# Attention and gated MLP on one core: earlier places in the queues for attention's sums, x's casts and the root's first step

## The chip, the core and the metric

The kernel runs on one core of a Trainium2 chip. Its time is the device time of one launch in microseconds (us). The core has a TensorE (PE, with a queue of weight loads PEld beside the matmuls), a VectorE (DVE), a ScalarE (ACT), a GpSimd (POOL) and a SyncE (SP), which issues the transfers. Each engine carries out its own instructions strictly in order; they wait for each other by semaphores. So the order in which instructions stand in an engine's queue is all that this change can act on.

## The reference

```python
# attention: B, H, S, D = 8, 8, 576, 64; two kinds of sparse causal mask
scores = np.where(masks, scale * q @ k.T, -1e9)      # window 32, or 32 keys at a distance of 4
attn = np.exp(scores - max); attn = attn / (sum + 1e-09)
x = (attn @ v)  ->  4608 tokens x 512
# MLP
rms = np.sqrt(np.mean(x * x, axis=-1, keepdims=True) + 1e-06)
xn = x / rms * rms_g
g = xn @ w_gate                                       # 512 x 1536
silu = g * (1.0 / (1.0 + np.exp(-g)))
return silu * (xn @ w_val) @ w_out                    # 1536 x 512
```

## The kernel before

The 4608 tokens are cut into 16 units `u` of 288 tokens. The MLP of a unit goes through 12 blocks `j` of 128 hidden columns. Each block has three **ticks**: the gate tick (PE: `g`, 12 matmuls), the val tick (PE: `v`, 12 matmuls) and the proj tick (PE: the products of the block before with `w_out`, 12 matmuls into `acc`). A unit is thus a stage of 36 ticks, about 67 us. Twelve matmuls stand for four products, since every operand is held as a sum of a rounded high part and a low part in fp32r and three of the four partial products are taken; this is why there are pairs `xhi, xlo`, `hhi, hlo`, `vhl`, `pt[:, 0], pt[:, 1]`.

Attention for unit u + 1 runs in the gaps of unit u's MLP. It has 14 bursts (a block of queries of two heads) per unit, one every second tick. A burst passes through: scores `s` on PE; maximum on DVE (`scores_max`, L379 and L384); exponential on ACT (L395); sum and reciprocal on DVE (L404, L405); scaling on GpSimd (L411); transpose `t` on PE (L482); the transposed probabilities are cast to a high part on ACT (L462) and their low part is taken on DVE (`low_part`, L464); product with v on PE (`o`, L494); and `take` (L432, L434, twice) sums the partial outputs on DVE into `xraw`.

PE's order in a tick is: the tick's 12 matmuls, then the products of attention (`o` first, then `t`, then `s`). What the other engines do with a tick's results is put off by `later(dt, rank, fn)` to the start of a tick dt ticks on, where `flush` carries out all that is due there in the order of the ranks. So a smaller rank means a place further ahead in the engines' queues, within one tick. `now[0]` counts the ticks; `ends` is the number of the first tick of the MLP, which is a proj tick, so `(now[0] - ends) % 3 == 0` names proj ticks. The argument `wait` of `products` is 1 in gate ticks, 2 in val ticks and 0 in proj ticks: what was issued in a proj tick is worked on at the start of the next gate tick.

PSUM is scarce: `g` and `v` of successive blocks alternate between two banks, and a transpose shares one with them. A transpose of a proj tick lies in the bank of `g` of its block j, and that is also the bank of `v` of block j + 1:

```python
    def bank(kind, j):
        return "gv"[(j + (kind == "v")) % 2]
```

So PE may write `v` of block j + 1 only when both ACT (L462) and DVE (L464) have read that transpose. Likewise a transpose of a val tick lies in the bank of that block's `g`, and PE may write it only when DVE's silu (`th` L690) has read `g`. `th` itself has a single buffer: ACT's tanh (L685) of a block waits until GpSimd has made `hlo` of the block before (L715).

At the end of a unit's attention `rms_sum` adds up squares on PE, `rms_root` makes 1/rms (DVE L559, then on GpSimd L560 the power, L565 and L566 the two parts), `spread` puts the parts on diagonals (`rd`, DVE L574 and ACT L578), and `rms_apply` broadcasts them by two matmuls into `bps` (L594). Then for each of four 128-row chunks c, `normal` scales x (DVE L608), and `part` splits it (ACT L625 `xhi`; low part L626 `xlo`, on GpSimd for even c and on DVE for odd c). The parts of chunks 0 and 3 fall into proj ticks.

Of the kernel before, what the change touches and what calls it, by code (L numbers as in the profile page):

```python
# [29 lines left out]
NEX = 3  # L30
# [46 lines left out]
def attn_moe(ctx: ExitStack, tc: tile.TileContext, qk_in, v_in, w_gate, w_val, w_out, rms_g, outT):  # L77
# [38 lines left out]
    now = [0]  # L116
    put_off = {}

    def later(dt, rank, fn):
        put_off.setdefault(now[0] + dt, []).append((rank, fn))  # L120
# [294 lines left out]
    def take(u, c, i, o):  # L415

        blocks, nq, _ = geometry(u, c)
        if (u, c) not in xraw:
            xraw[u, c] = sb.tile([P, U], F32, tag="xraw", name=f"xraw_{u}_{c}", bufs=NC)
        x = xraw[u, c]  # L420
        if c < NC // 2:
            to = x[:, QB * i:QB * i + nq]
        else:
            to = x.rearrange("p (j r) -> p r j", r=DIL)[:, i, :]
        copy = V.tensor_copy if i % 2 and u == 0 and c == NC - 1 else A.copy
        if u < NEX:
            for a in range(2):
                copy(out=to[a * D:(a + 1) * D], in_=o[a * D:(a + 1) * D, a * nq:(a + 1) * nq])
        else:
            for a in range(2):  # L430
                ours, cols = to[a * D:(a + 1) * D], 2 * a * nq
                V.tensor_reduce(out=ours, in_=o[:D, cols:cols + 2 * nq].rearrange("d (t q) -> d q t", t=2),  # L432
                                axis=mybir.AxisListType.X, op=ALU.add)
                V.tensor_tensor(out=ours, in0=o[D:, cols:cols + nq], in1=ours, op=ALU.add)  # L434
        if i == len(blocks) - 1:
            dt = 1 if c != 1 or u < NEX else 4
            later(dt, 0.44 if u >= NEX and (now[0] + dt - ends) % 3 == 0 else 2.5 if u else 1.9, lambda: square(u, c))
# [31 lines left out]
    def products(q, t, o, t_ps, s_tag="s", o_tag="o", wait=0):  # L469


        if q:
            s_ps = ps.tile([P, 512], F32, tag=s_tag, name=f"s_{q[0]}_{q[1]}_{q[2]}")
        if o:
            o_ps = ps.tile([P, 512], F32, tag=o_tag, name=f"o_{o[0]}_{o[1]}_{o[2]}")
            pt = st.pop(o)
        if t:
            p, _ = st.pop(t)
        def transposed(a):
            blocks, nq, _ = geometry(*t[:2])  # L480
            n = blocks[t[2]][3]
            PE.transpose(t_ps[:n, a * QB:a * QB + nq], p[:nq, a, :n], ident[:nq, :nq])  # L482

        def output(a):
            blocks, nq, _ = geometry(*o[:2])
            n = blocks[o[2]][3]
            if o[0] < NEX:
                if a:
                    return
                out = o_ps[:, :2 * nq].rearrange("d (a q) -> d a q", a=2)  # L490
                PE.matmul(out, vs.pop(o)[:n].rearrange("k a d -> k (a d)"), pt[:n, 0, :, :nq], start=True, stop=True)
                return
            vp = vparts[everything.index(o) % 2]
            PE.matmul(o_ps[:, 2 * a * nq:2 * (a + 1) * nq].rearrange("d (t q) -> d t q", t=2),  # L494
                      vp[:n, a].rearrange("k t d -> k (t d)"), pt[:n, :, a, :nq], start=True, stop=True)

        def scored(a):
            blocks, nq, _ = geometry(*q[:2])
            qc, kc, _, n = blocks[q[2]]
            sv = s_ps[:QB].rearrange("q (a t k) -> q a t k", a=2, t=2)  # L500
            if q[0] < NEX:
                qk = heads[q[0], 2 * q[1] + a]
                PE.matmul(sv[:nq, a, 0, :n], qk[:, qc:qc + nq], qk[:, U + kc:U + kc + n], start=True, stop=True)
                return
            qs, ks = heads[q[0], 2 * q[1] + a]
            PE.matmul(sv[:nq, a, :, :n], qs[:, qc:qc + nq], ks[:, :, kc:kc + n], start=True, stop=True)  # L506

        order = ((t, transposed), (o, output), (q, scored))
        if t and t[0] >= NEX:
            order = ((o, output), (t, transposed), (q, scored))  # L510
        parts = [(b, fn, a) for b, fn in order for a in range(2)]
        for b, fn, a in parts:
            if b:
                fn(a)
        if t:
            later(1, 0.2, lambda: untranspose(t, t_ps, wait))
        if o:
            later(1, 0.5 if o[0] < NEX else 0.55, lambda: take(*o, o_ps))
            if o[0] < NEX:
                later(1, 9, lambda: load_v(further(o, 3)))  # L520
            far = further(o, 2)
            if far and far[0] >= NEX:
                split_v(far, 8 if o[0] < NEX else 1)
        if q:
            later(1, 0.7, lambda: scores_max(*q, s_ps))
            later(2, 0.42 if wait == 1 else 2, lambda: scores_exp(*q))
            later(3 if q[0] < NNAT else 4, -1, lambda: scores_norm(*q))
            u, c, i = q
            nxt = after(u, 2 * c, 2)
            nb = len(geometry(u, c)[0])  # L530
            if u < NEX:
                if u == NNAT - 1 and c == NC - 1 and i == nb - 1:
                    for h in range(4):
                        later(1, 9, lambda h=h: load(NNAT, h))
                if u >= NNAT and i == nb - 1 and c < NC - 1:
                    for a in range(2):
                        later(1, 9, lambda a=a: load(*after(u, 2 * c + a, 4)))
                if u == NEX - 1 and c == NC - 1 and i == nb - 1:
                    for a in range(2):
                        later(3 + a, 9, lambda a=a: split(NEX, a, (1, 2, 2, 3), G, G))  # L540
            elif nxt and i == 0:
                split(*nxt, (1, 2, 2, 3), G, G)
                split(nxt[0], nxt[1] + 1, (2, 3, 3, 4) if c < NC - 1 else (1, 2, 3, 4), G, G)
# [5 lines left out]
    def rms_sum(u):  # L549
        r_ps = ps.tile([QB, NB, 2], F32, tag="o", name=f"rps_{u}")  # L550
        for i in range(NB):
            PE.matmul(r_ps[:, i, :], xsq[u][:, i * QB:(i + 1) * QB], inv, start=True, stop=True)
        later(1, 0.1, lambda: rms_root(u, r_ps))
        if u == 0:
            later(1, 6, spread_first)

# [33 lines left out]
    def rms_apply(u):  # L590
        ds = rst.pop(u)
        b_ps = ps.tile([P, U], F32, tag="o", name=f"bps_{u}")
        for k, d in enumerate(ds):
            PE.matmul(b_ps, (ones if u else ones32)[:QB, :], d.rearrange("p i q -> p (i q)"),  # L594
                      start=k == 0, stop=k == len(ds) - 1)
        xs[u] = {}
        if u == 0:
            root.append(sb.tile([P, U], F32, tag="tmp", name="root", bufs=2))
            later(1, 0.62, lambda: V.tensor_copy(out=root[0], in_=b_ps))

        def normal(c):
            x = xraw[u, c]
            if u == 0:
                xn = sb.tile([P, U], F32, tag="xhi", name=f"xn_{c}", bufs=4)
                V.tensor_tensor(out=xn, in0=x, in1=b_ps, op=ALU.mult)
                xs[u][c] = xn
                return
            V.scalar_tensor_tensor(out=x, in0=x, scalar=gs[:, c:c + 1], in1=b_ps,  # L608
                                   op0=ALU.mult, op1=ALU.mult)

        def part(c):
            x = xraw.pop((u, c))
            k = (u * NC + c) % 6
            if u > 1 and not spare:
                spare.append(cst.tile([P, 3, U], F32R, tag=f"slot{state['free']}", name="spare"))
            if k == 5 and u > 1:
                hi = spare[0][:, 2]
            else:
                pool, tag, bufs = (sb, "xhi", 4) if k < 4 else (late[0], ("xhi", "ot")[k - 4], 1)
                hi = pool.tile([P, U], F32R, tag=tag, name=f"xhi_{u}_{c}", bufs=bufs)  # L620
            if c < 2 and u % 2 == 0:
                lo = spare[0][:, c]
            else:
                lo = late[0].tile([P, U], F32R, tag=f"xlo{c // 2}", name=f"xlo_{u}_{c}", bufs=2)
            A.copy(out=hi, in_=x)  # L625
            (V if c % 2 else G).tensor_tensor(out=lo, in0=x, in1=hi, op=ALU.subtract)  # L626
            xs[u][c] = (hi, lo)

        for c in range(NC):
            later((1, 2, 2, 3)[c] if u else 1, 0.6 + (0.03 * (c > 1) if u == 0 else 0), lambda c=c: normal(c))  # L630
            if u:
                later((2, 3, 4, 5)[c], 0.6, lambda c=c: part(c))


    hs, acc, gv = {}, {}, {}
# [153 lines left out]
    ends = nb + LAG + OUT + 5  # L789
# [127 lines left out]
```

## Time and profile before

| | us |
|---|---|
| median of 3 runs (1122.04 to 1126.86) | 1122.29 |
| the profiled execution | 1124.24 |
| its span in the trace | 1122.5 |
| PE busy | 1105.5 (98%) |
| PEld busy | 1074.1 (96%) |
| DVE busy | 782.8 (70%) |
| GpSimd busy | 671.7 (60%) |
| ACT busy | 618.8 (55%) |

A row of the trace's timeline gives the start from the span's beginning in us, the duration in us, the engine, the line of the code, the operation, the tiles written and read, and in brackets the engine's idle time just ahead of the instruction and what ended it. [...] A row of the list of waits gives: who waited, for whom, the time in total, how often, and the longest.

### The profile page before, as it was taken

The numbers are of one execution on the slowest core, as the hardware profiler recorded it, in microseconds if no ns is written. First come the engines' busy times: TensorE is split into PE (matmuls) and PEld (weight loads), VectorE is DVE, ScalarE is ACT, GpSimd is POOL, SyncE is SP. The second block draws the span as 40 slices with busy tenths as digits, with TensorE's granted clock in tenths as the row PEclk, the third lists the DMA queues.
The fourth block names the chain that finished last, engine by engine and source line by source line (L and its number), as shares of the span: only waits on it lengthen the run. The fifth ranks groups of instructions, "written<-read, shape, count | busy, mean of one in ns | idle before, by whom it ended". The sixth has DMA issues, their size and how long they took to land.

```text
span 1122.5 us, 25515 instructions
## 1 busy us (share of the span) xinstructions
PE 1105.5 (98%) x8362; PEld 1074.1 (96%) x8362; DVE 782.8 (70%) x3098; ACT 618.8 (55%) x2215; POOL 671.7 (60%) x1154
## 2 busy tenths in 40 slices
PE   8999999999999999999999999999999999999998
PEld 6787999999999999999999999999999999999998
DVE  6889667867677686876767677686767767677412
ACT  6695576546465564646546465564646556464211
POOL 6423578756576575756657575675657657584211
PEclk9899999999999999999999999999999999999999
DMA  9665212212131131311212121131312212120000
GB/s 249 181 227 214 72 43 87 83 36 78 42 92 52 34 91 42 92 41 50 86 39 84 41 83 53 47 93 28 88 43 70 73 32 80 46 79 14 7 16 22
DMA packets 61543, 82.18 MB, mean 73 GB/s; under 512 B 7298, under 2 KB 41090, under 8 KB 61410
## 3 DMA queue, kind: packets, MB, share of 16 engines
q1 hardware_dynamic: 61410, 80.54, 23.9%
q8 instruction: 67, 1.10, 0.4%
q14 instruction: 66, 0.54, 0.2%
HBM read 71.08 MB, written 9.44 MB: 72 GB/s over the span
## 4 chain that ended last, share of the span: by engine, by line
PE 76%; DVE 12%; ACT 5%; POOL 3%; issue 2%; DMA 1%; SPq 0%; DVEq 0%; POOLq 0%; ACTq 0%
PE acc L648 14%; PE g L648 14%; PE v L648 12%; PE acc L645 7%; PE g L645 7%; PE v L645 6%; PE o L494 2%; PE acc L642 2%; DVE t L384 2%; PE s L506 2%; PE v L642 2%; PE t L482 2%; PE g L642 2%; DVE th L690 2%; DVE xraw L432 2%
## 5 line engine op out<-in xcount | busy, mean ns | idle before, releaser
L715 POOL TENSOR_TENSOR hlo<-th,hhi 128x288 fp32r<-128x288 f32 x179 | 145.8, 815 | 163.0 <-ACT hhi L714 149.5
L395 ACT ACTIVATE t<-t,sum 96x128 f32<-96x128 f32 (+3 forms) x448 | 166.1, 373 | 125.0 <-DVE sum L384 123.4
L648 PE MATMUL acc<-hhi,lo 128*128 128x288 f32 x720 | 212.7, 295 | 0.0
L411 POOL TENSOR_SCALAR t<-t,sum 72x72 f32<-72x72 f32 (+3 forms) x414 | 149.7, 373 | 99.0 <-DVE sum L405 84.7
L648 PE MATMUL g<-xhi,lo 128*128 128x288 f32 x612 | 180.2, 295 | 0.0
L648 PE MATMUL v<-xhi,lo 128*128 128x288 f32 x612 | 180.2, 294 | 0.0
L685 ACT ACTIVATE th<-g 128x288 f32<-128x288 f32 x180 | 73.6, 409 | 184.4 <-PE g L648 92.6
L432 DVE TENSOR_REDUCE xraw<-o 64x72 f32<-64x144 f32 (+1 forms) x364 | 116.3, 320 | 68.1 <-PE o L494 65.6
L690 DVE SCALAR_TENSOR_TENSOR th<-th,g 128x288 f32<-128x288 f32 x180 | 80.8, 449 | 87.3 <-ACT th L685 63.3
L648 PEld LDWEIGHTS acc<-hhi,lo 128*128 128x128 f32 x720 | 135.4, 188 | 0.0
L323 POOL TENSOR_TENSOR vhl<-vt,vhl 128x128 fp32r<-128x128 f32 x182 | 84.2, 463 | 72.7 <-ACT vhl L319 69.8
L714 ACT CAST hhi<-th 128x288 fp32r<-128x288 f32 x180 | 77.8, 432 | 77.4 <-DVE th L703 77.2
L648 PEld LDWEIGHTS g<-xhi,lo 128*128 128x128 f32 x612 | 115.2, 188 | 0.0
L648 PEld LDWEIGHTS v<-xhi,lo 128*128 128x128 f32 x612 | 115.1, 188 | 0.0
L434 DVE TENSOR_TENSOR xraw<-o,xraw 64x72 f32<-64x72 f32 (+1 forms) x364 | 100.9, 277 | 12.5
L645 PE MATMUL acc<-hhi,hi_o 128*128 128x288 f32 x360 | 109.0, 303 | 0.0
L703 DVE TENSOR_TENSOR th<-th,v 128x288 f32<-128x288 f32 x180 | 79.8, 444 | 39.7 <-PE v L648 35.5
L645 PE MATMUL g<-xhi,hi_g 128*128 128x288 f32 x357 | 107.0, 300 | 0.0
L648 PE MATMUL acc<-hlo,hi_o 128*128 128x288 f32 x360 | 106.5, 296 | 0.0
L362 POOL TENSOR_TENSOR qs<-qk,qs 64x288 fp32r<-64x288 f32 x104 | 84.3, 810 | 23.6 <-ACT qs L357 16.3
L648 PE MATMUL g<-xlo,hi_g 128*128 128x288 f32 x322 | 95.1, 295 | 0.0
L353 POOL TENSOR_TENSOR ks<-qk,ks 128x288 fp32r<-128x288 f32 (+2 forms) x104 | 93.2, 901 | 3.1
(186 smaller groups left out, 3482.1 us busy)
## 6 DMA issues: line engine op xcount, KB each, us to landing
qk<-in_qk_dram SPq DMA_DIRECT2D x60, 288.0 KB, 2.9
vt<-in_v_dram SPq DMA_DIRECT2D x196, 64.0 KB, 1.9
qk<-in_qk_dram SPq DMA_DIRECT2D x30, 352.0 KB, 3.1
out_dram<-ot SPq DMA_DIRECT2D x64, 144.0 KB, 2.0
qk<-in_qk_dram SPq DMA_DIRECT2D x30, 304.0 KB, 2.8
raw<-in_w_gate_dram SPq DMA_DIRECT2D x12, 512.0 KB, 4.3
raw<-in_w_val_dram SPq DMA_DIRECT2D x12, 512.0 KB, 4.3
raw<-in_w_out_dram SPq DMA_DIRECT2D x12, 512.0 KB, 4.1
```

Of the source, the lines that this page charges most:

```text
L323: G.tensor_tensor(out=vp[:, :, 1], in0=vs.pop(b), in1=vp[:, :, 0], op=ALU.subtract)
L353: ek.tensor_tensor(out=ks[:, 1, :nkt], in0=kr, in1=ks[:, 0, :nkt], op=ALU.subtract)
L362: eq.tensor_tensor(out=qs[D:], in0=qr[D:], in1=qs[D:], op=ALU.subtract)
L395: A.activation(out=t[:nq, a, :n], in_=t[:nq, a, :n], func=AF.Exp, scale=-1.0, bias=sm[:nq, a, 0:1], accum_out=sm[:nq, a, 1:2] if u or i % ...
L411: (V if u == 0 and (c, i) > (NC - 1, 0) else G).tensor_scalar(out=t[:nq, a, :n], in0=t[:nq, a, :n], scalar1=sm[:nq, a, 3:4], scalar2=1.0, ...
L432: V.tensor_reduce(out=ours, in_=o[:D, cols:cols + 2 * nq].rearrange("d (t q) -> d q t", t=2), axis=mybir.AxisListType.X, op=ALU.add)
L434: V.tensor_tensor(out=ours, in0=o[D:, cols:cols + nq], in1=ours, op=ALU.add)
L645: PE.matmul(out, wh[:, cc, :], xh, start=start, stop=False)
L648: PE.matmul(out, w[:, cc, :], v, start=False, stop=stop and k == 1)
L690: V.scalar_tensor_tensor(out=t, in0=t, scalar=1.0, in1=g, op0=ALU.add, op1=ALU.mult)
L703: V.tensor_tensor(out=t, in0=t, in1=v_ps[:, :U], op=ALU.mult)
L715: (V if (u, j) == (NU - 1, NJ - 1) else G).tensor_tensor(out=lo, in0=t, in1=hi, op=ALU.subtract)
```

## The change

Three ranks are changed. No instruction is added or removed.

```diff
@@ products @@
         if o:
-            later(1, 0.5 if o[0] < NEX else 0.55, lambda: take(*o, o_ps))
+            later(1, 0.5 if o[0] < NEX else 0.55 if wait else 0.1, lambda: take(*o, o_ps))
@@ rms_sum @@
-        later(1, 0.1, lambda: rms_root(u, r_ps))
+        later(1, -1.2 if u > 1 else 0.1, lambda: rms_root(u, r_ps))
@@ rms_apply @@
             if u:
-                later((2, 3, 4, 5)[c], 0.6, lambda c=c: part(c))
+                dt = (2, 3, 4, 5)[c]
+                later(dt, 0.45 if u > 1 and (now[0] + dt - ends) % 3 == 0 else 0.6, lambda c=c: part(c))
```

The orders of PE and of SP stay as they were; those of DVE, ACT and GpSimd change at the following places of each stage from unit 2's on. (The new file is one line longer from L632 on, so L690, L703 and L714 to L715 of before are L691, L704 and L715 to L716 there.)

**DVE, from unit 5's last silu product to the first gate tick of unit 6** (`th` L703 is the last product of the old unit, `xlo` the low part of chunk 3, `pt` the low part of the transposed probabilities, `xraw` the sums of attention's outputs, `t` L379 the next scores). Before:

```order
L703 TENSOR_TENSOR th_11_6772<-th_11_6772,v_11_6791 128x288
L626 TENSOR_TENSOR xlo_3_6817<-xraw_3_6400,xhi_3_6816 128x288
L464 TENSOR_TENSOR pt_0_2_6844<-t_11_6835,pt_0_2_6844 128x192
L432 TENSOR_REDUCE xraw_0_6847<-o_0_0_6837 64x96
L434 TENSOR_TENSOR xraw_0_6847<-o_0_0_6837,xraw_0_6847 64x96
L432 TENSOR_REDUCE xraw_0_6847<-o_0_0_6837 64x96
L434 TENSOR_TENSOR xraw_0_6847<-o_0_0_6837,xraw_0_6847 64x96
L379 TENSOR_TENSOR t_1_2_6852<-s_1_2_6836,mask 96x256
```

And now:

```order
L704 TENSOR_TENSOR th_11_6772<-th_11_6772,v_11_6791 128x288
L626 TENSOR_TENSOR xlo_3_6813<-xraw_3_6400,xhi_3_6812 128x288
L432 TENSOR_REDUCE xraw_0_6844<-o_0_0_6837 64x96
L434 TENSOR_TENSOR xraw_0_6844<-o_0_0_6837,xraw_0_6844 64x96
L432 TENSOR_REDUCE xraw_0_6844<-o_0_0_6837 64x96
L434 TENSOR_TENSOR xraw_0_6844<-o_0_0_6837,xraw_0_6844 64x96
L464 TENSOR_TENSOR pt_0_2_6849<-t_11_6835,pt_0_2_6849 128x192
L379 TENSOR_TENSOR t_1_2_6852<-s_1_2_6836,mask 96x256
```

The four instructions of `take` have moved ahead of the low part. The same happens in the gate ticks of blocks 2, 4 and 6 of each stage, where no `xlo` stands ahead of them: four places per stage.

**ACT, in the proj tick just ahead of that** (`hhi` is the high part of the old unit's last h, `xhi` that of x's chunk 3). Before:

```order
L357 CAST qs_5_6788<-qk_5_6636 128x288
L395 ACTIVATE t_1_1_6781,sum_88<-t_1_1_6781,sum_88 96x128 x2
L714 CAST hhi_11_6812<-th_11_6772 128x288
L625 CAST xhi_3_6816<-xraw_3_6400 128x288
L462 CAST pt_0_2_6844<-t_11_6835 128x192
```

And now:

```order
L357 CAST qs_5_6788<-qk_5_6636 128x288
L395 ACTIVATE t_1_1_6781,sum_88<-t_1_1_6781,sum_88 96x128 x2
L625 CAST xhi_3_6812<-xraw_3_6400 128x288
L715 CAST hhi_11_6816<-th_11_6772 128x288
L462 CAST pt_0_2_6849<-t_11_6835 128x192
```

The cast of x no longer stands behind that of h. In the proj tick of block 10 the same swap is made for chunk 0, there with GpSimd's `hlo` and `xlo` swapped as well.

**GpSimd, in the proj tick of block 9** (`ks` belongs to a later head, `t` is a burst's probabilities to be scaled, `rst` the root). Before:

```order
L353 TENSOR_TENSOR ks_3_6565<-qk_3_6192,ks_3_6565 128x320
L411 TENSOR_SCALAR t_0_0_6539<-t_0_0_6539,sum_89 96x128 x2
L560 TENSOR_TENSOR rst_6622<-rst_6622,mhalf 96x3
L565 CAST rst_hi_6625<-rst_6622 96x3
L566 TENSOR_TENSOR rst_lo_6626<-rst_6622,rst_hi_6625 96x3
L715 TENSOR_TENSOR hlo_9_6632<-th_9_6586,hhi_9_6631 128x288
```

And now:

```order
L353 TENSOR_TENSOR ks_3_6565<-qk_3_6192,ks_3_6565 128x320
L560 TENSOR_TENSOR rst_6617<-rst_6617,mhalf 96x3
L565 CAST rst_hi_6620<-rst_6617 96x3
L566 TENSOR_TENSOR rst_lo_6621<-rst_6617,rst_hi_6620 96x3
L411 TENSOR_SCALAR t_0_0_6539<-t_0_0_6539,sum_89 96x128 x2
L716 TENSOR_TENSOR hlo_9_6632<-th_9_6586,hhi_9_6631 128x288
```

The three steps of the root have moved ahead of the scaling. On DVE the root's first step (L559) has moved ahead of L404, L405 and L703 of that tick.

## Prediction

> **What bounds the kernel now.** I read the busy shares first, then the list of waits of PE's two queues, then the timeline around each wait.
>
> ```profile
> span 1122.5 us, 25515 instructions
> PE 1105.5 (98%) x8362; PEld 1074.1 (96%) x8362; DVE 782.8 (70%) x3098; ACT 618.8 (55%) x2215; POOL 671.7 (60%) x1154
> ```
>
> PE is busy 1105.5 of 1122.5 us, and neither its instructions nor their order change. So only PE's waits can be won or added to; a wait of DVE, ACT or GpSimd counts only where PE waits behind it. In the waits of the weight loads, and one of DVE, three rows bear on the change:
>
> ```profile
> PEld t L482 <- DVE th L690: 6.6, 19, 0.6
> PEld bps L594 <- ACT rd L578: 4.8, 13, 0.6
> DVE pt L464 <- ACT pt L462: 35.2, 39, 1.0
> ```
>
> PE waits 6.6 us for silu ahead of transposes in val ticks, and 4.8 us for the root's diagonals. Together 11.4 us, 1.0% of the span, is all there is to win. DVE idles 0.9 us in each of 39 gate ticks for ACT's cast of the transpose while `take` could run; PE meets that only through silu.
>
> **The root's first step.** Rows around one of the 13 waits for `rd`:
>
> ```profile
> 445.01 0.86 POOL L353 TENSOR_TENSOR ks<-qk,ks 128x320 fp32r<-128x320 f32 x1
> 446.01 0.71 POOL L411 TENSOR_SCALAR t<-t,sum 96x128 f32<-96x128 f32 x2
> 446.69 0.86 POOL L560 TENSOR_TENSOR rst<-rst,mhalf 96x3 f32<-96x3 f32 x1
> 448.38 0.91 ACT L578 ACTIVATE rd<-ident,rst_lo 96x96 fp32r<-96x96 f32 x3 [1.65 <-POOL rst_lo L566]
> 448.85 0.30 PE L594 MATMUL bps<-rd,ones 96*128 96x288 f32 x1
> 449.33 0.19 PEld L594 LDWEIGHTS bps<-rd,ones 96*128 96x128 f32 x1 [0.43 <-ACT rd L578]
> 449.57 0.30 PE L645 MATMUL v<-xhi,hi_o 128*128 128x288 f32 x1
> ```
>
> GpSimd ends `ks` at 445.87 and could start the power some 0.08 us later, if DVE's L559, now first in its tick, is through by then: 445.95 in place of 446.69, 0.74 us sooner. `rd` would end at 448.55 instead of 449.29; PE wants the second weight load at 448.85. The wait goes, with 0.25 us to spare: 4.8 us in all. What is late next is the scaling of `t` (446.01) by the root's three steps, about 1.5 us, but its transpose comes two ticks on (3.7 us). L404, L405 and L703 slip by the short L559; PE reads what hangs on them a block later. I take nothing for these.
>
> The same rows price a held weight load, which I need below: the load was due at 448.85 with the matmul ahead of it and came at 449.33, 0.48 late; `v` came at 449.57 where two steps of 0.13 (a load runs one such step ahead of its matmul, 472.26 and 472.39 below) would have put it at 449.11, so PE lost 0.46. A late weight load costs its lateness less about 0.02.
>
> **`take` ahead of the low part, blocks 2, 4 and 6 (39 places).** Block 2 of one stage:
>
> ```profile
> 470.23 0.37 PE L494 MATMUL o<-pt,vhl 128*128 128x192 f32 x2
> 471.15 0.36 DVE L464 TENSOR_TENSOR pt<-t,pt 128x192 fp32r<-128x192 f32 x1 [0.84 <-ACT pt L462]
> 471.43 0.34 DVE L432 TENSOR_REDUCE xraw<-o 64x96 f32<-64x192 f32 x1
> 472.46 0.26 DVE L434 TENSOR_TENSOR xraw<-o,xraw 64x96 f32<-64x96 f32 x1
> 472.75 0.37 DVE L379 TENSOR_TENSOR t<-s,mask 72x208 f32<-72x208 f32 x1
> 472.26 0.19 PEld L645 LDWEIGHTS v<-xhi,hi_o 128*128 128x128 f32 x1
> 472.39 0.29 PE L645 MATMUL v<-xhi,hi_o 128*128 128x288 f32 x1
> ```
>
> `o` is ready at 470.60, so `take` starts at 470.64 and lasts 1.29 (471.43 to 472.72). The low part follows 0.03 later (as L379 follows L434 here) and takes 0.36: it ends at 472.31. DVE is free for L379 about 0.5 us sooner than before, and so is silu. That removes those of the 19 waits for silu that lie in these blocks. But the low part now ends 0.8 us later than at 471.51, and `v` of this block must not overwrite the transpose before. Its weight load is due at 472.26; with 0.05 us from DVE's end to PE (row 462.84 below) it can go at 472.36. So a **new wait of 0.1 us** arises: PE on the low part, with all of PE's queue behind it. Block 6 is tighter, for no scores follow its transposes:
>
> ```profile
> 492.95 0.34 PE L494 MATMUL o<-pt,vhl 104*128 104x144 f32 x2
> 493.77 0.31 DVE L464 TENSOR_TENSOR pt<-t,pt 104x144 fp32r<-104x144 f32 x1 [0.79 <-ACT pt L462]
> 494.00 0.29 DVE L432 TENSOR_REDUCE xraw<-o 64x72 f32<-64x144 f32 x1
> 494.97 0.29 DVE L434 TENSOR_TENSOR xraw<-o,xraw 64x72 f32<-64x72 f32 x1
> 494.77 0.19 PEld L645 LDWEIGHTS v<-xhi,hi_o 128*128 128x128 f32 x1
> ```
>
> `o` ends 493.29, plus 0.04, 1.26, 0.03, 0.31 and 0.05 is 494.98 against 494.77: 0.21 late. Block 4 has the widths of block 6 but scores behind its transposes (about 0.15 us more): 0.07 late. Less 0.02 each: 0.09 + 0.05 + 0.19 = 0.33 us lost per stage.
>
> **Block 0 (13 places), where the cast of x counts.**
>
> ```profile
> 457.75 0.19 ACT L395 ACTIVATION_READ_ACCUMULATOR t<-t,sum 96x1 f32 x1
> 458.14 0.43 ACT L714 CAST hhi<-th 128x288 fp32r<-128x288 f32 x1 [0.21 <-DVE th L703]
> 458.30 1.08 POOL L353 TENSOR_TENSOR ks<-qk,ks 128x416 fp32r<-128x416 f32 x1
> 458.34 0.37 PE L494 MATMUL o<-pt,vhl 128*128 128x192 f32 x2
> 458.48 0.43 ACT L625 CAST xhi<-xraw 128x288 fp32r<-128x288 f32 x1
> 458.94 0.76 DVE L626 TENSOR_TENSOR xlo<-xraw,xhi 128x288 fp32r<-128x288 f32 x1 [0.83 <-ACT xhi L625]
> 460.42 0.19 PEld L645 LDWEIGHTS v<-xhi,hi_g 128*128 128x128 f32 x1
> 461.09 0.41 ACT L685 ACTIVATE th<-g 128x288 f32<-128x288 f32 x1 [1.66 <-POOL hlo L715]
> 462.36 0.43 DVE L690 SCALAR_TENSOR_TENSOR th<-th,g 128x288 f32<-128x288 f32 x1
> 462.84 0.20 PEld L482 LDWEIGHTS t<-ident,t 96*128 96x128 f32 x2 [0.52 <-DVE th L690]
> ```
>
> Here is one of the longest of the 19 waits, 0.52 us. DVE is busy without a gap from `xlo` to silu, so `xlo`'s start counts. Ahead of `hhi`, `xhi` need not wait: ACT takes in an instruction 0.09 ahead of the end of the one before (458.48 against 458.57), so `xhi` starts at 457.85, ends 458.28, and `xlo` can start at 458.31, 0.03 behind it as before. That is within 0.01 us of GpSimd's start of `ks`, and the two disturb each other:
>
> ```profile
> 453.90 0.66 POOL L411 TENSOR_SCALAR t<-t,sum 96x128 f32<-96x128 f32 x1
> 453.97 0.44 DVE L626 TENSOR_TENSOR spare<-xraw,xhi 128x288 fp32r<-128x288 f32 x1
> 185.92 0.46 POOL L323 TENSOR_TENSOR vhl<-vt,vhl 128x128 fp32r<-128x128 f32 x1
> 186.00 0.70 DVE L626 TENSOR_TENSOR spare<-xraw,xhi 128x288 fp32r<-128x288 f32 x1
> ```
>
> Undisturbed, L626 takes 0.44. With `ks` well under way (458.94 row) it ends 0.32 behind the end of `ks` (459.38), whenever it began. At 453.97 DVE started 0.07 behind GpSimd and was not held, while L411 took 0.66 instead of 0.37; at 186.00, 0.08 behind, DVE was held. With both starting together I take DVE first: `xlo` 458.31 to 458.75, `take` from 458.74 (`o` ready at 458.71), low part done at 460.41 and to PE at 460.46, against 460.42: 0.04 late, 0.02 lost. Silu moves ahead by up to 0.88 us; what comes last then is tanh, which waits for `hlo` (461.09) and may slip 0.13 with GpSimd: silu from 461.67 is through to PE by 462.15. PE's load, held for 0.52 behind the load ahead, would have started 0.09 before that one's end, at 462.23. The wait goes. Between the ends (DVE first, GpSimd first) I take the first, since the row with the nearest distance short of holding, 0.07, is still DVE's.
>
> [...]
>
> In the proj tick of block 10 the swapped cast delays `hlo` by about 0.8 us; its readers, tanh of the next block and proj, come over 1 us later. Nothing. In the first of the 13 stages `ks` started 0.26 us behind the accumulator's read, not 0.55:
>
> ```profile
> 190.16 0.18 ACT L395 ACTIVATION_READ_ACCUMULATOR t<-t,sum 96x1 f32 x1
> 190.42 1.08 POOL L353 TENSOR_TENSOR ks<-qk,ks 128x416 fp32r<-128x416 f32 x1
> ```
>
> `xlo` would come at 190.71, 0.3 us behind `ks`, and be held: 0.9 us lost there, as priced under rival 1.
>
> **The sum.** Won: 4.8 + 6.6 = 11.4. Lost: 13 stages x (0.33 + 0.02) = 4.6, and 0.9 for the first. Net 5.7 us won. The profiled execution took 1124.24 (span 1122.5, 1.74 around it), 0.2% above the median of 1122.29; it would take 1118.5. Against the median: **1116.5 us**, 0.5% less.
>
> **Rivals.** (1) *GpSimd is first and `xlo` gains nothing; slower.* Then `xlo` ends at 459.70 as before, `take` runs 459.62 to 460.91, and the low part ends at 461.29 against a weight load at 460.42: 0.9 us lost where 0.02 was; in the stages whose `ks` is narrower, and so shorter (0.86 us at 128x320 in row 445.01, 1.08 at 128x416), some 0.3 less. Twelve stages of 0.75 on average: 9 us, so 1125.5. It decides from about 8 of the 12 places on. For it: the casts leave `xlo` no lead over `ks`. Against: 453.97.
> (2) *The low part does not hold `v`.* If the wait held the matmul instead of the weight load, there would be 0.13 us more time and only block 6 would lose 0.1: 11.4 - 1 - 1 = 9.4, so 1113. Against: at 449.33 it is the weight load that waits.
> (3) *Silu stays late.* If tanh comes last more often than I think, half of the 6.6 stays: 1120. For it: tanh's margin at 462.15 is 0.08 us.
>
> **Chances.** Forecast 0.50 (1114.5 to 1118.5), (1) 0.20 (1121 to 1126), (2) 0.12 (1111 to 1114), (3) or a mixture of places 0.18 (1118 to 1121). I call no change what lies within 0.5% (5.6 us, so above 1116.7), about what can be told apart here. Half of the forecast's mass and (2) are faster by more: 0.40; slower by more than 0.5% only if (1) comes with further waits: 0.04; the rest 0.56. The range 1112.5 to 1122.5 holds the forecast, (3), half of (2) and a third of (1).
>
> **What would show it.** PE's waits for `rd` L578 gone; for `th` L690 gone or below 1 us; new rows of PEld `v` waiting for DVE `pt` L464, some 40 times, 4 to 6 us in total, longest in block 0 of the first stage; DVE's wait for ACT `pt` gone. L626 on DVE at 0.44 in block 0 says DVE came first; at over 1 us, rival 1. A `v` held for 0.6 us or more in most stages would make the forecast wrong.

## The result and the profile after

| | before | after |
|---|---|---|
| median, us | 1122.72 of 4 runs (1122.04 to 1126.86) | 1114.20 of 4 runs (1113.16 to 1115.96) |
| profiled execution, span | 1122.5 | 1112.9 |

The ratio is 0.9918 (95% interval 0.989 to 0.9946): 8.5 us less. The forecast was 1116.5; the time lies inside its range, 2.3 us below the forecast and 0.3 below its band (1114.5 to 1118.5). It is faster by more than 0.5%, which had a chance of 0.40; "no change" had 0.56.

The page's first lines of after:

```profile
span 1112.9 us, 25461 instructions
PE 1098.3 (99%) x8362; PEld 1071.1 (96%) x8362; DVE 783.9 (70%) x3098; ACT 613.5 (55%) x2215; POOL 674.9 (61%) x1154
```

For the same 8362 matmuls PE's busy time fell by 7.2 us and its idle time by 2.4 (17.0 to 14.6): a part of what PE waits counts as busy, as the held matmul of block 6 below shows (0.40 us, where the free ones around it are 0.29 to 0.30). In after's list of waits (who waited, for whom, total us, times, longest) there is no row any more for `t` behind silu, none for `bps` behind `rd`, and none for DVE's `pt` behind ACT's. What is there instead:

```profile
DVE xraw L432 <- PE o L494: 80.1, 103, 1.8
...
PEld v L646 <- DVE pt L464: 2.9, 11, 1.3
...
PE v L646 <- DVE pt L464: 1.0, 1, 1.0
...
PEld v L646 <- DVE sum L404: 0.5, 3, 0.2
```

DVE now waits for `o` in 39 more places than before (103 against 64), and PE waits for the low part. The list shows 14 of these waits of the load only, 3.4 us in all: 11 put down to the low part, and 3 in the same place of block 6 put down to the `sum` that DVE takes up as the low part ends. It leaves out the short ones, as the single matmuls show: PE's order is unchanged, so each matmul of after can be set beside the same one of before, and the difference of their starts, followed down the queue, jumps wherever one of them waited. From 175 us on, where the change begins to act, the jumps above 0.025 us are:

| place | matmuls | us |
|---|---|---|
| `t` behind `o` (was held by silu) | 32 | +7.6 |
| the second `t` behind it | 33 | +1.3 |
| `bps` and the `v` behind it (was held by `rd`) | 26 | +5.2 |
| `v`, the first two matmuls of gate ticks 0, 2, 4, 6 | 66 | -6.6 |
| all smaller jumps | | +0.1 |
| sum | | **+7.6** |

The other 2.1 us by which the profiled spans differ arise ahead of 175 us, where the change does nothing yet; the experiments come back to that.

### The profile page after: what moved, and what is told of

Same layout as the page of the kernel before. It is cut to its first block, busy times and chain, and to the rows that moved or that the text cites. A ratio compares the mean times of both kernels' runs of the same rounds, so it can differ in the third digit from the quotient of the medians.

```text
span 1112.9 us, 25461 instructions
## 1 busy us (share of the span) xinstructions
PE 1098.3 (99%) x8362; PEld 1071.1 (96%) x8362; DVE 783.9 (70%) x3098; ACT 613.5 (55%) x2215; POOL 674.9 (61%) x1154
## 3 DMA queue, kind: packets, MB, share of 16 engines
q8 instruction: 66, 1.08, 0.4%
## 4 chain that ended last, share of the span: by engine, by line
PE 92%; DMA 3%; POOL 2%; DVE 1%; ACT 1%; issue 0%; SPq 0%; POOLq 0%; DVEq 0%; ACTq 0%
PE acc L649 17%; PE g L649 16%; PE v L649 16%; PE v L646 9%; PE acc L646 9%; PE g L646 8%; PE o L494 3%; PE s L506 3%; PE acc L643 2%; PE v L643 2%; PE g L643 2%; PE t L482 2%; DMA v<-in_v_dram 2%; PE g L482 1%; DMA raw<-in_w_gate_dram 1%; PE s L503 1%
## 5 line engine op out<-in xcount | busy, mean ns | idle before, releaser
L716 POOL TENSOR_TENSOR hlo<-th,hhi 128x288 fp32r<-128x288 f32 x179 | 145.8, 814 | 149.6 <-ACT hhi L715 129.5
L411 POOL TENSOR_SCALAR t<-t,sum 72x72 f32<-72x72 f32 (+3 forms) x414 | 148.0, 369 | 83.1 <-DVE sum L405 71.0
L691 DVE SCALAR_TENSOR_TENSOR th<-th,g 128x288 f32<-128x288 f32 x180 | 81.0, 450 | 102.4 <-ACT th L686 78.0
L715 ACT CAST hhi<-th 128x288 fp32r<-128x288 f32 x180 | 77.7, 432 | 74.5 <-DVE th L704 73.6
L704 DVE TENSOR_TENSOR th<-th,v 128x288 f32<-128x288 f32 x180 | 79.9, 444 | 55.1 <-PE v L649 55.0
L353 POOL TENSOR_TENSOR ks<-qk,ks 128x288 fp32r<-128x288 f32 (+2 forms) x104 | 96.8, 936 | 3.1
```

The costliest lines, as they stand in the source:

```text
L353: ek.tensor_tensor(out=ks[:, 1, :nkt], in0=kr, in1=ks[:, 0, :nkt], op=ALU.subtract)
L411: (V if u == 0 and (c, i) > (NC - 1, 0) else G).tensor_scalar(out=t[:nq, a, :n], in0=t[:nq, a, :n], scalar1=sm[:nq, a, 3:4], scalar2=1.0, ...
L691: V.scalar_tensor_tensor(out=t, in0=t, scalar=1.0, in1=g, op0=ALU.add, op1=ALU.mult)
L704: V.tensor_tensor(out=t, in0=t, in1=v_ps[:, :U], op=ALU.mult)
L716: (V if (u, j) == (NU - 1, NJ - 1) else G).tensor_tensor(out=lo, in0=t, in1=hi, op=ALU.subtract)
```

## The places in after's trace

The root, block 9 of a stage (start, us, engine, line, operation):

```profile
441.36 0.87 POOL L353 TENSOR_TENSOR ks<-qk,ks 128x320 fp32r<-128x320 f32 x1
442.18 0.86 POOL L560 TENSOR_TENSOR rst<-rst,mhalf 96x3 f32<-96x3 f32 x1
443.82 0.71 POOL L411 TENSOR_SCALAR t<-t,sum 96x128 f32<-96x128 f32 x2
443.87 0.91 ACT L578 ACTIVATE rd<-ident,rst_lo 96x96 fp32r<-96x96 f32 x3 [0.73 <-POOL rst_lo L566]
445.05 0.32 PEld L594 LDWEIGHTS bps<-rd,ones 96*128 96x128 f32 x2
445.45 0.30 PE L646 MATMUL v<-xhi,hi_o 128*128 128x288 f32 x1
```

The power starts with the end of `ks`; `rd` is done at 444.78, the second of the two loads that share the 445.05 row goes at 445.18, and nothing holds it. The scaling of `t` comes 1.64 us behind the power's start, and PE meets none of that.

Block 0:

```profile
453.72 0.42 ACT L625 CAST xhi<-xraw 128x288 fp32r<-128x288 f32 x1
454.04 0.43 ACT L715 CAST hhi<-th 128x288 fp32r<-128x288 f32 x1
454.17 0.46 DVE L626 TENSOR_TENSOR xlo<-xraw,xhi 128x288 fp32r<-128x288 f32 x1 [0.17 <-ACT xhi L625]
454.20 1.37 POOL L353 TENSOR_TENSOR ks<-qk,ks 128x416 fp32r<-128x416 f32 x1
454.63 0.35 DVE L432 TENSOR_REDUCE xraw<-o 64x96 f32<-64x192 f32 x1
455.96 0.36 DVE L464 TENSOR_TENSOR pt<-t,pt 128x192 fp32r<-128x192 f32 x1
456.38 0.19 PEld L646 LDWEIGHTS v<-xhi,hi_g 128*128 128x128 f32 x1
457.08 0.41 ACT L686 ACTIVATE th<-g 128x288 f32<-128x288 f32 x1 [1.76 <-POOL hlo L716]
457.52 0.45 DVE L691 SCALAR_TENSOR_TENSOR th<-th,g 128x288 f32<-128x288 f32 x1
458.22 0.21 PEld L482 LDWEIGHTS t<-ident,t 96*128 96x128 f32 x2
```

`xlo` starts 0.03 us ahead of GpSimd's `ks`, takes 0.46 us, and now it is `ks` that pays: 1.37 us where it took 1.08. In all twelve such stages `xlo` led by 0.002 to 0.031 us and took 0.46. The low part ends at 456.32 and `v`'s load goes at 456.38, 0.07 late. Silu starts right behind tanh, ends at 457.97, and the transposes' loads at 458.22 are free.

Block 6, where the new wait is longest:

```profile
488.43 0.30 DVE L432 TENSOR_REDUCE xraw<-o 64x72 f32<-64x144 f32 x1 [0.34 <-PE o L494]
489.73 0.31 DVE L464 TENSOR_TENSOR pt<-t,pt 104x144 fp32r<-104x144 f32 x1
490.10 0.19 PEld L646 LDWEIGHTS v<-xhi,hi_o 128*128 128x128 f32 x1 [0.17 <-DVE pt L464]
490.10 0.40 PE L646 MATMUL v<-xhi,hi_o 128*128 128x288 f32 x1
```

The load comes 0.22 us after it was due, which is with the start of `g`'s last matmul. The matmul that uses it and the next one were 0.10 and 0.11 us later against before: 0.20 for a lateness of 0.22. So the price of this held load is its lateness less 0.02, and it falls on two matmuls; in blocks 0, 2 and 4, where the load is late by 0.05 to 0.14, one matmul shows it.

The first stage, where `xlo` was not early enough:

```profile
187.91 1.09 POOL L353 TENSOR_TENSOR ks<-qk,ks 128x416 fp32r<-128x416 f32 x1
188.22 1.10 DVE L626 TENSOR_TENSOR xlo<-xraw,spare 128x288 fp32r<-128x288 f32 x1 [0.18 <-ACT spare L625]
190.97 0.19 PEld L646 LDWEIGHTS v<-xhi,hi_g 128*128 128x128 f32 x1 [1.25 <-DVE pt L464]
```

It started 0.30 behind `ks` and ended 0.31 behind its end. PE lost 1.28 us at `v`, and got 0.63 back at the transpose two ticks on, which silu held in before.

## The experiments

The theory: three parts act one by one on PE's queue. Root's step takes away PE's wait for `rd`. `take` ahead of the low part takes away the wait for silu, and puts up a new one, `v` for the low part. The cast's place decides by who starts first, `xlo` or `ks`, whether that new wait is small or eats all that `take` won. The first rival: the cast is of no weight and the gain is root's and take's. The second: `ks` lengthened on GpSimd costs as much as `xlo` wins. Ratios are to runs of before on the same chip, whose median was 1122.12 us in the first four experiments and 1122.85 in the last three.

| kernel | median, us | ratio | jumps from 175 us on: silu, root, `v` |
|---|---|---|---|
| root_only | 1117.49 | 0.9960 (0.9947 to 0.9973) | 0, +5.2, 0 |
| no_cast | 1123.47 | 1.0009 (1.0000 to 1.0019) | +8.9, +5.2, -15.1 |
| late_cast | 1123.48 | 1.0011 (1.0002 to 1.0020) | +8.9, +5.2, -15.1 |
| split_take | 1109.10 | 0.9886 (0.9871 to 0.9901) | +8.9, +5.2, 0 |
| cast_only | 1119.48 | 0.9979 (0.9966 to 0.9992) | +2.5, 0, 0 |
| split_nocast | 1115.02 | 0.9930 (0.9918 to 0.9943) | +3.2, +5.2, -1.9 |
| near_cast | 1123.76 | 1.0004 (0.9995 to 1.0013) | +8.9, +5.2, -15.3 |

**root_only**: before, with the root's rank alone.

```diff
-        later(1, 0.1, lambda: rms_root(u, r_ps))
+        later(1, -1.2 if u > 1 else 0.1, lambda: rms_root(u, r_ps))
```

> Only the root's step is moved ahead. Matched matmul for matmul, the changed kernel against the one before shows 5.2 us less ahead of PE's second root matmul and of v behind it, in 13 places. If these waits are independent of the others, this kernel keeps exactly that: 13 waits for rd gone, the waits for th L690 (6.6 us in the list) as before, no new wait of v; 5 us off, about 1117.5 against 1122.5. Rival: the time won at the root only moves PE into the next wait (silu of the same block, or GpSimd's scaling that was pushed back); then under 2 us are left and new waits for POOL t L411 show.

Its waits have no row for `bps`; silu's stands as it was:

```profile
PEld t L482 <- DVE th L690: 6.8, 20, 0.6
```

So root's part is worth 5.2 us by itself, the same jumps that it gives in the changed kernel, and it touches nothing else.

**no_cast**: the changed kernel with the cast of x at its old place.

```diff
-                dt = (2, 3, 4, 5)[c]
-                later(dt, 0.45 if u > 1 and (now[0] + dt - ends) % 3 == 0 else 0.6, lambda c=c: part(c))
+                later((2, 3, 4, 5)[c], 0.6, lambda c=c: part(c))
```

> Root and take as in the changed kernel, but the cast of x stays behind that of h. Theory: in block 0 xlo starts 0.6 us later, while GpSimd's ks runs, is held to its end, and take ahead of the low part then lets the low part end 0.9 us after v's weight load is due (0.65 us in the stages with the narrower ks): 12 places lose about 0.75 more than in the changed kernel, 9 us in all, so about 1123, no better than before. Rival: take alone brings the gain and the cast is idle; then 1114 to 1116 and v in block 0 waits under 0.2 us.

From its timeline in block 0, and its waits:

```profile
456.40 1.08 POOL L353 TENSOR_TENSOR ks<-qk,ks 128x416 fp32r<-128x416 f32 x1
457.04 0.75 DVE L626 TENSOR_TENSOR xlo<-xraw,xhi 128x288 fp32r<-128x288 f32 x1 [0.83 <-ACT xhi L625]
459.04 0.36 DVE L464 TENSOR_TENSOR pt<-t,pt 128x192 fp32r<-128x192 f32 x1
459.45 0.19 PEld L645 LDWEIGHTS v<-xhi,hi_g 128*128 128x128 f32 x1 [0.89 <-DVE pt L464]
```

```profile
PEld v L645 <- DVE pt L464: 11.5, 22, 0.9
```

`xlo` starts 0.64 behind `ks`, and `v`'s load is 0.94 to 0.97 late in the stages with a 416-wide `ks`, 0.65 to 0.69 in those with a 288-wide one. Silu no longer holds PE, but PE pays more at `v` than it had won at silu. So `take`'s new place loses without the cast: 8.9 - 15.1 = -6.2 us, and root's 5.2 leaves -1.0 of that. The first rival falls.

**late_cast**: the changed kernel, and on ACT ahead of the early cast of chunk 3 a second write of the ones that `ones` holds already (0.28 us), to let `ks` start first without moving anything else.

```diff
+            if c == NC - 1 and u > 1:
+                A.copy(out=ones, in_=one.to_broadcast([P, P]))
             A.copy(out=hi, in_=x)
```

> The changed kernel with one more ACT instruction (the constant ones written again, 128x128) ahead of xhi of chunk 3 in each unit from 2 on, so that xlo starts about 0.17 us after GpSimd's ks instead of just ahead of it. If the two exclude each other and the first keeps the port, xlo takes about 1.2 us (0.9 in the narrower stages) instead of 0.46, ks takes 1.08 (0.80) again instead of 1.38 (1.10), and PE's v of block 0 waits 0.9 (0.65) us: about 9 us lost against the changed kernel, 1123. Rival: no exclusion, DVE is only 0.2 us later: xlo takes 0.46, v waits 0.25 us, 2 to 3 us lost, 1117.

```profile
455.71 1.07 POOL L353 TENSOR_TENSOR ks<-qk,ks 128x416 fp32r<-128x416 f32 x1
...
455.89 1.22 DVE L628 TENSOR_TENSOR xlo<-xraw,xhi 128x288 fp32r<-128x288 f32 x1 [0.37 <-ACT xhi L627]
```

`xlo` starts 0.17 to 0.19 behind `ks` and takes 1.20 to 1.23 us in the wide stages; `ks` is back at 1.07 to 1.08. `v` loses the same 15.1 us as without the early cast. So 0.2 us in the cast's end turn the whole of the cast's gain, which is the start order and not the cast's place as such. The second rival falls too: with `ks` undisturbed the kernel is the slower one. That it is a port which the first one keeps, as I expected, was not shown: the rows show who started first and how long each took.

**near_cast**: as late_cast, with 8 columns in place of 128.

```diff
-                A.copy(out=ones, in_=one.to_broadcast([P, P]))
+                A.copy(out=ones[:, :8], in_=one.to_broadcast([P, 8]))
```

> The changed kernel with a write of ones ahead of the early cast as in late_cast, of 8 columns in place of 128, so shorter: xlo starts behind ks by less than late_cast's 0.18 us, an estimate 0.05 to 0.12. Theory (whoever starts first holds the other off): xlo takes 0.8 to 1.2 us wherever it starts behind ks, and v is held as in late_cast, 1123; the changed kernel's lead was only 2 to 31 ns, so this much is enough to turn all 12 places. Rival: a start some tens of ns behind still goes through, xlo takes 0.46 and ks is the one lengthened, 1114 to 1115. A mixture by place would show where the border lies.

```profile
455.86 0.18 ACT L626 CAST ones<-one 128x8 fp32r<-128x8 f32 x1
...
456.32 1.08 POOL L353 TENSOR_TENSOR ks<-qk,ks 128x416 fp32r<-128x416 f32 x1
456.40 1.31 DVE L628 TENSOR_TENSOR xlo<-xraw,xhi 128x288 fp32r<-128x288 f32 x1 [0.28 <-ACT xhi L627]
```

Now `xlo` is 0.070 to 0.094 behind, and still held in all twelve places (1.30 to 1.32 us in the wide stages, 1.03 to 1.05 in the others), to 0.31 or 0.32 us behind the end of `ks`. The rival that a start some tens of ns behind goes through falls for this pair of instructions; where between 0.002 ahead, the smallest lead in the changed kernel, and 0.07 behind the border lies, no run shows.

**cast_only**: before, with the cast's rank alone.

```diff
-                later((2, 3, 4, 5)[c], 0.6, lambda c=c: part(c))
+                dt = (2, 3, 4, 5)[c]
+                later(dt, 0.45 if u > 1 and (now[0] + dt - ends) % 3 == 0 else 0.6, lambda c=c: part(c))
```

> The cast of x ahead of h's alone; the low part stays ahead of take, and root where it was. Theory: xlo of the last chunk starts ahead of ks and takes 0.46 us, but the low part behind it now waits for ScalarE's pt, which in the 416-wide stages of before ended 0.36 us ahead of the low part's start (459.23 against 459.62) and in the 288-wide ones 0.11 (526.48 against 526.59). So silu comes 0.36 and about 0.1 us earlier at block 0 alone: 6 x 0.36 + 6 x 0.1 = 2.8 us, about 1119.5 us; v is never held. Had the cast its worth by itself, as much as it is worth beside take (9 us between no_cast and the changed kernel), this would be at 1113; were it worth nothing by itself, 1122.

```profile
455.25 1.36 POOL L353 TENSOR_TENSOR ks<-qk,ks 128x416 fp32r<-128x416 f32 x1
455.85 0.32 ACT L462 CAST pt<-t 128x192 fp32r<-128x192 f32 x1 [0.33 <-PE t L482]
456.20 0.36 DVE L464 TENSOR_TENSOR pt<-t,pt 128x192 fp32r<-128x192 f32 x1 [0.53 <-ACT pt L462]
...
459.43 0.20 PEld L482 LDWEIGHTS t<-ident,t 96*128 96x128 f32 x2 [0.17 <-DVE th L691]
```

`ks` took 1.36 us, as where `xlo` led in the changed kernel (1.37 to 1.40 in the wide stages) and not 1.08, so DVE was first, and the low part then idles 0.53 us for ACT's `pt`. Silu still holds the transpose, by 0.17 where it was 0.52. The jumps are +2.5 us at 12 places, where 2.8 were expected. That 1119.48 met the 1119.5 so closely is in part luck, for before's median was 1122.85 here and the forecast had counted from 1122.3. Alone the cast is worth 2.5 us; beside `take` it is worth 8.5 (15.1 - 6.6). The gain of the two together is not the sum of the two alone: -6.2 and +2.5 would make -3.7, and they make +2.3 (8.9 - 6.6).

**split_take**: the changed kernel, with the low part between the two heads of `take`. The last argument names the heads to be summed; the lines of `take` that read it are left out here.

```diff
-            later(1, 0.5 if o[0] < NEX else 0.55 if wait else 0.1, lambda: take(*o, o_ps))
+            if o[0] >= NEX and not wait:
+                later(1, 0.1, lambda: take(*o, o_ps, (0,)))
+                later(1, 0.25, lambda: take(*o, o_ps, (1,)))
+            else:
+                later(1, 0.5 if o[0] < NEX else 0.55, lambda: take(*o, o_ps))
```

> The changed kernel, but in gate ticks the low part stands between the two halves of take (head 0, low part, head 1). Theory: the new wait of v (6.6 us in the matched matmuls, of it 1.3 in the first stage) comes only from the low part standing behind all of take; now the low part ends about 0.6 us sooner, 0.4 ahead of v's need, and DVE is free for the next scores no later than in the changed kernel. So v's waits go in all places but the first stage (0.4 left there), the gains at silu (8.9) and at the root (5.2) stay: 6 us under the changed kernel, about 1108.5. Rival: the low part then waits for ACT's cast again and silu gets late: waits for th L690 come back, 1112 to 1114.

Its timeline in block 0:

```profile
452.72 0.46 DVE L630 TENSOR_TENSOR xlo<-xraw,xhi 128x288 fp32r<-128x288 f32 x1 [0.18 <-ACT xhi L629]
452.74 1.39 POOL L353 TENSOR_TENSOR ks<-qk,ks 128x416 fp32r<-128x416 f32 x1
...
453.86 0.36 DVE L464 TENSOR_TENSOR pt<-t,pt 128x192 fp32r<-128x192 f32 x1
454.24 0.35 DVE L432 TENSOR_REDUCE xraw<-o 64x96 f32<-64x192 f32 x1
...
454.85 0.19 PEld L650 LDWEIGHTS v<-xhi,hi_g 128*128 128x128 f32 x1
```

One head of `take` (0.64 us) is enough to fill DVE's wait for ACT's `pt`; the low part ends at 454.21 and `v`'s load at 454.85 is held by nothing. Its waits have no row of `v` behind `pt` and none of `t` behind silu. All that silu and root give stays, 14.4 us in the jumps, with nothing to pay; the medians show 13.0 of it, and where the other 1.4 went no run shows. In the first stage too `xlo` (189.09, 0.46 us) came 0.02 ahead of `ks`, so the loss that I expected there did not come; why it came ahead here is open. This is the fastest of all the kernels: 1109.10 us (1108.89 to 1109.47), 13 us below before and 5 below the changed kernel.

**split_nocast**: the same with the cast at its old place.

> As split_take (the low part between take's two heads), but the cast of x left at its old place. Theory: xlo stays blocked by ks (0.75 us, from 0.64 behind it), which held v in block 0 by 0.95 us in the 416-wide stages of no_cast and 0.66 in the 288-wide ones; with take's second head (0.63) behind the low part that leaves 0.3 and 0.03 us, at 6 or 7 places 0.28 us: about 2 us lost against split_take's 1109.1, so 1111. Rival: with the split the cast is worth nothing, 1109; or worth all of what it was worth in the changed kernel (9 us), 1118.

Its waits:

```profile
PEld t L482 <- DVE th L694: 5.3, 13, 0.6
...
PEld v L649 <- DVE pt L464: 1.7, 7, 0.2
```

And from its timeline in block 0:

```profile
457.89 0.43 DVE L694 SCALAR_TENSOR_TENSOR th<-th,g 128x288 f32<-128x288 f32 x1
...
458.37 0.20 PEld L482 LDWEIGHTS t<-ident,t 96*128 96x128 f32 x2 [0.39 <-DVE th L694]
```

The `v` side came as expected, 7 places and 1.9 us. But silu is back, 13 places in block 0: by the medians the kernel takes 5.9 us more than split_take, by the jumps it loses 7.6 (5.7 at silu, 1.9 at `v`), where I had forecast 2. The step that I left out: the held `xlo` delays everything on DVE behind it. In no_cast that delay was paid at `v`, which held PE for 0.95 us, and silu then had that much more time; here `v`'s load is at most 0.31 us late, and what is left of the delay meets PE at silu (0.39 us in the rows). So in these two kernels PE pays for DVE's delay at the first place that it meets, and what it has waited there is not asked again behind it.

**The start.** In the table of jumps root_only gains 5.2 us, and its median is 4.6 below before's; the changed kernel gains 7.6 and its median is 8.5 below. Between profiled spans the difference is larger by 1.4 to 2.6 us in all kernels but split_take (0.5), and all of that lies ahead of 175 us. Rows of 20 to 40 us of the span, for before, after and split_take, in that order (busy us and counts of PE, PEld, DVE, ACT, POOL, then the granted clock, DMA's share and GB/s):

```profile
20.00:40.00 20.00, 17.95 (x94) 13.94 (x92) 14.63 (x60) 13.28 (x52) 11.95 (x20) 0.83 0.84 207
```

```profile
20.00:40.00 20.00, 17.25 (x107) 13.83 (x108) 17.02 (x69) 13.79 (x53) 13.16 (x21) 1.00 0.88 215
```

```profile
20.00:40.00 20.00, 17.98 (x94) 14.02 (x92) 15.00 (x57) 13.20 (x49) 11.85 (x19) 0.83 0.81 206
```

At a granted clock of 0.83, 94 matmuls were done in these 20 us; at 1.00, 105 to 107. The profiled executions of before and split_take had that piece at the lower clock; after, no_cast, cast_only and near_cast (1.00) had none; root_only, late_cast and split_nocast (0.91) had half of it. Between 20 and 40 us, matmul against matmul, the four at 1.00 gain 2.4 to 2.7 us on before, the three at 0.91 gain 1.5 to 1.9, and split_take gains nothing. The orders of PE, DVE, ACT and GpSimd are the same there, so this comes and goes between executions and is no part of the change. In before's trace the clock is 0.76, 0.50, 0.50 and 0.53 in the four pieces of 2 us from 26 to 34 us and 1.00 in the other pieces of 2 us; its clock records have 6.83 us at 0.50, from 27.04 to 33.87, which makes the mean of 0.83 over the 20 us. A mean of 0.91, if it comes of a clock of 0.50 too, is 3.6 us of it: an estimate from before's record, about half of before's 6.83.

## Why the prediction was right, and where it was off

- **Root: right.** 4.8 forecast, 5.2 in the jumps, confirmed alone by root_only. `ks` to power without a gap, `rd` early by 0.40 us against the 0.25 forecast. Nothing was late next.
- **Silu: the mechanism right, the term mis-sized.** 6.6 forecast, 8.9 measured. The forecast took the row of the list as all there was to win. It holds the 19 longest waits of the load, and these are 6.6 us in the jumps too; the list leaves out 13 more of 0.05 to 0.10 us (1.0 us), and the 0.04 us that the second transpose lost behind each (1.3). The sentence "11.4 us is all there is to win" was wrong: split_take won 14.4.
- **The low part holds `v`: right in kind, 1.1 us too small.** 4.6 + 0.9 forecast, 6.6 measured: the load was late by 0.07 to 0.09, 0.10 to 0.14, 0.05 to 0.11 and 0.21 to 0.24 us in blocks 0, 2, 4 and 6 against 0.04, 0.10, 0.07 and 0.21, which costs about 0.06 us per stage more, 0.7 us in all; and the first stage cost 1.28. The price of a late load, its lateness less 0.02, held. Rival 2 falls: it is the load that waits.
- **What would show it: one sign misread.** The row of `v` was to show some 40 waits and 4 to 6 us. It shows 14 and 3.4 (3 of them put down to `sum`), of which 1.25 is the first stage's; the rest are below what the list counts, as with silu.
- **Block 0, DVE or `ks` first: right, on a wrong reason.** The forecast put `xlo` 0.01 behind `ks` and took DVE first because L626 had not been held 0.07 behind L411. near_cast shows that 0.07 behind `ks` it is held, every time. It came out well by luck: `xlo` led after all, by 0.002 to 0.031. L411 has one SBUF tensor to read (and a column of factors), `ks` two; the row was of another kind of instruction, though that this is why was not tried. Rival 1's price was about right: 9 us forecast, and 8.5 to 8.7 more lost at `v` in no_cast, late_cast and near_cast, where GpSimd was first. Its time was 1125.5 against 1123.5 to 1123.8, for silu's term was too small there too. For `xlo` against `ks` the records have: first by 0.002 to 0.031 us, 12 of 12 not held (0.46); behind by 0.07 to 0.09 (near_cast) or 0.17 to 0.19 (late_cast), 25 of 25 held to beyond the end of `ks`.
- **Silu stays late (rival 3): no.** Tanh did come last, as forecast, and silu 0.03 behind it; the transposes' loads were met in all stages. The forecast had a free load start 0.09 us ahead of the end of the load before it; those of `t` between 400 and 600 us of after's span started 0.05 to 0.06 ahead, so tanh's margin was about 0.03 us wider than the 0.08 that the forecast gave it.
- **The sum.** The terms as stated give 5.9, and the text took 5.7. Measured: 8.9 + 5.2 - 6.6 + 0.1 = 7.6 us in the jumps, 8.5 between the medians. Of the 2.8 us by which the gain was larger than forecast, silu's term gives 2.3, root's 0.4 and `v`'s -1.1; 0.1 are small jumps, 0.2 the slip in the sum, and 0.9 lie outside the jumps, within the spread of the runs (2.8 us from the lowest to the highest of after) and of the start. The median of before is 0.4 higher here than the one that the forecast started from, so the time is 2.3 below it.

## What to carry to other kernels

Where one engine sets the time and its order is fixed, set its instructions before and after side by side, one by one: the list of waits is right about the long ones and silent about many short ones (here 2.3 of 8.9 us won, and about half of the 6.6 lost). When a piece of work is moved to fill another's wait, move as much as the wait holds and no more: half of `take` filled DVE's idle time, the other half only pushed the low part past its due time, and splitting it was worth 5 us over the change itself. And a part that loses alone can be the condition of the gain: `take` lost 6.2 us and the cast alone won 2.5, but the two together won 2.3, on a lead of `xlo` of 0.03 us at most, so try the parts together and know the margin.

## What the runs showed of the hardware that I had not expected

- Between DVE's subtraction `xlo` (128x288) and GpSimd's `ks` (128x416 in the times that follow), each of two SBUF tensors, some tens of nanoseconds in the start decided all: with DVE first by 0.002 to 0.031 us DVE took 0.46 and GpSimd 1.37 instead of 1.08; with GpSimd first by 0.07 us GpSimd took 1.08 and DVE 1.31 instead of 0.46. Here that is more than 9 us of a kernel's time (1114.20 against 1123.76).
- The held one of these two did not just wait for the rest of the other: `xlo` ended 0.31 to 0.32 us after the end of `ks`, whether it started 0.07, 0.18 or 0.30 behind, though it takes 0.44 when nothing holds it; and `ks` was lengthened by 0.29 to 0.32 when `xlo` has 0.46 to run. So either was held by some 0.13 us less than the records would have it if nothing of the two overlapped; why, no run shows.
- In block 6 a matmul whose load was late by 0.22 us passed half of it to the next: 0.10 and 0.11 us on two matmuls, where one is listed as waiting.
